# Two first blocks transposed on quarters of the array, and v's conversion moved from GpSimd to VectorE, in a fused attention and MoE kernel

## The chip, the core and the metric

The kernel runs on one core of a Trainium2 chip. The metric is the device time of one execution in microseconds (us), as a median of runs; lower is better. Before the change the three runs gave 338.6, 339.99 and 340.03 us, so the median is 339.99 us.

The engines are named as in the profile: PE is TensorE's matmul, PEld its weight load, DVE is VectorE, ACT is ScalarE, POOL is GpSimd, SP is SyncE, which here only issues DMAs. "SPq" and "POOLq" are the queues of these engines.

## The reference, cut to what matters

q, k and v have 8 batches, 8 heads, 576 positions and 64 channels; f holds forget gates. Attention with a decay is followed by a feed-forward layer of 512 to 2048 to 512 (called MoE in the code):

```python
log_f = np.log(np.clip(f, 0.0001, 1.0))
cum = np.cumsum(log_f, axis=-1)
scores = scale * q @ k.T + cum[:, :, :, None] - cum[:, :, None, :]   # causal
attn = softmax(scores)
x = (attn @ v).transpose(0, 2, 1, 3).reshape(4608, 512)
h = x @ w_in
out = (h * (1.0 / (1.0 + np.exp(-h)))) @ w_out
```

The decay factors into a weight for each key, so the kernel multiplies every row of v (and a column of ones beside it, for the sum of the softmax) by exp(-cum), shifted by half the last sum. That product is what the text calls the conversion of v: it reads fp32 and writes bf16, and it is needed before attention of its batch.

## The kernel before, in words

**Blocks.** A batch's 576 positions are cut into a first block of 128 positions, three blocks of 128 and a tail of 64. First blocks of all 8 batches are done first (a prologue), the rest in the last loop of the kernel, over 16 rounds (`for m in range(NQ)`, L980). This text calls a round a quad; it holds two pairs of heads, n = 2m and 2m + 1, so two quads make a batch: an even one and an odd one. Batch b is attended in quads 2b and 2b + 1.

**First blocks (L131 to L398).** `load_qk0` (L131) has GpSimd load q and k of one first block and cast them to bf16 on the way, one DMA for each, over 128 partitions: a partition holds a run of 8 positions of one head. `turn0` (L285) transposes them with matmuls against a selection matrix `sel` (L293): for q and then for k, 8 positions times 2 halves of heads, 16 matmuls of 64 columns into a PSUM tile of tag "big", each with 128 rows and 64 output partitions. ACT copies q's result out, DVE copies k's (L300). `two_more` (L855) does two first blocks, 4 and 5, then 6 and 7, between pieces of the MoE work. `out0` and `back0` finish a first block.

**The rest.** `load_qk`, `load_tails` and `load_v` (L155 to L194) issue loads, mostly on SP; `load_v(b, c)` loads v's block c + 1 of batch b, so its c = 0 is the first block of the rest, into one of four fp32 buffers vf (L190). `cast_qk` (L402) casts q on POOL, `transposes` (L439) transposes by DMA on SP (L443), and `convert_v(b, c)` (L418) does the conversion of v on POOL (L429): one instruction of 128x520 for c = 0, 1 and 2, and two of 64x260 for c = 3. Each result goes into one of two buffers vp, which take turns by batch.

**A quad (L980 to L1052).** `scores` (L460) computes scores and exponentials, `mask` and `mask_tail` (L490, L496) multiply by triangles on DVE (L492, L498), `attend` (L506) multiplies by v (L522, L531) and DVE normalises (L539, L540). `turn(n)` casts and transposes a later pair and calls `prepare` (L907), which issues the loads of v of the next batch in the even quad and its conversions in the odd quad.

**MoE work in between.** `m1_chunk` (L576) is one chunk hp of the first matmul (4 matmuls L583), followed by a tanh on ACT (L591) and the product gt on DVE (L592). `m2_part` (L610) is a quarter of a row block of the second matmul, po (L628). `m2_rows` (L645) does a whole row block, pr, in row pairs (L654) in two halves, and `m2_fence` (L663) puts a one-column copy of pr on DVE between them (L665); the second half of pr waits for it. All of hp, po, pr, the attention's dn and the transposes share four PSUM buffers of tag "big", which go round in the order of the program; the scores have two buffers of tag "sc".

**The order** is written by hand: every engine runs its instructions in the program's order (`manual_schedule`, L54). `step` (L712) emits a chunk or a part, `wanted` (L695) chooses which, and `fill`, `slot`, `ones` and `rest` emit so many microseconds or so many steps of them.

Of the kernel before, what the change touches and what calls it, by code (L numbers as in the profile page):

```python
# [10 lines left out]
FP32 = mybir.dt.float32  # L11
BF16 = mybir.dt.bfloat16
P = 128
# [5 lines left out]
def kernel(  # L19
# [10 lines left out]
    nc = tc.nc  # L30

    B, H, S, D = q.shape
# [4 lines left out]
    NP = H // 2  # L37
    SM = 512
    ST = S - SM
    NM = SM // P  # L40
# [7 lines left out]
    RUN = 8  # L48
    NRUN = P // RUN
    assert D == 64 and S == 576 and DM == H * D and NP == NCC and B == 8  # L50
    assert NRUN * H == P
    scale = 1.0 / float(D) ** 0.5

    ctx.enter_context(tc.manual_schedule(engines=set(ORDERED)))  # L54
# [13 lines left out]
    psc = ctx.enter_context(tc.tile_pool(name="psc", bufs=2, space=bass.MemoryType.PSUM))  # L68
# [4 lines left out]
    w_bf = const.tile([P, NM + 1, BH], BF16, name="w_bf")  # L73
    ident_bf = const.tile([P, P], BF16, name="ident_bf")
    sel = const.tile([P, 2, D], BF16, name="sel")
    ident_f = const.tile([BH, BH], FP32, name="ident_f")
    tri = const.tile([P, P], BF16, name="tri")
    trit = const.tile([P, 2, ST], BF16, name="trit")
# [4 lines left out]
    kT0 = [const.tile([P, NP, P], BF16, name=f"kT0_{b}") for b in range(B)]  # L83
# [46 lines left out]

    def load_qk0(b):  # L131
        t = conv.tile([P, 2, RUN * D], BF16, name="qkb", tag="qkb")
        for i, src in enumerate((q, k)):
            nc.gpsimd.dma_start(
                out=t[:, i, :],
                in_=src[b, :, 0:P, :].rearrange("h (r c) d -> r h (c d)", c=RUN),
            )
        qk0[b] = t

    def load_v0(b):  # L140
# [277 lines left out]
    def convert_v(b, c):  # L418
        vbf[b] = vps[b % 2]
        if c < NR:  # L420
            parts = [(slice(0, P), slice(0, P), slice(0, H), slice(0, H))]
        else:
            parts = [
                (slice((1 - i) * ST, (2 - i) * ST), slice(ST, P), slice(0, NP), slice(i * NP, (i + 1) * NP))
                for i in range(2)
            ]
        for ro, r, ho, h in parts:
            w = w_bf[r, c + 1, b * H + h.start : b * H + h.stop, None]
            nc.gpsimd.tensor_tensor(  # L429
                out=vbf[b][ro, c, ho, :],  # L430
                in0=vst[b][c][r, h, :],
                in1=w.to_broadcast([r.stop - r.start, h.stop - h.start, D + 1]),
                op=ALU.mult,
            )
# [256 lines left out]
    lag = {"g": 1, "parts": 0}  # L691

    begin: dict[int, tuple[int, int]] = {}

    def wanted(a, c):  # L695

# [15 lines left out]
    def step(force=0):  # L712

        a, c = at["m1"], at["m2"]
        want = wanted(a, c)
        if not want:
            return None
        g1 = M1[a][0] if a < len(M1) else NG
        g2 = M2[c][0] if c < len(M2) else NG
        can1 = g1 in ready and not (M1[a][1] == 0 and g1 > g2 + lag["g"])  # L720
        can2 = open2["w"] and c < len(M2) and g2 < g1
        kind = force if (force == 1 and can1) or (force == 2 and can2) else want
        if kind == 1:
            if M1[a][1] == 0:
                begin[g1] = (0, c)
            m1_chunk(g1, M1[a][1])
            at["m1"] += 1
            t = 4 * (GW[g1] / 2.4 + 2.5)
        else:
            m2_part(*M2[c])  # L730
            at["m2"] += 1
            t = 4 * (DM / 2.4 + 2.5)
        return t

    def behind():
        t = sum(4 * (GW[g] / 2.4 + 2.5) for g, _ in M1[at["m1"] :] if g in ready)
        t += sum(4 * (DM / 2.4 + 2.5) for g, _, _ in M2[at["m2"] :] if g in ready)
        return t / 1000
# [91 lines left out]
        nc.gpsimd.memset(t[:, 0:NM, 1, :], 0.0)  # L830
    load_w_out(0)
    load_w_out(1)
    convert_v0(4)
    convert_v0(5)
    load_w_out(2)
    load_w_out(3)
    load_qk0(6)
    load_qk0(7)
    load_v0(6)
    load_v0(7)  # L840
# [11 lines left out]
    cast_qk(1)  # L852
    transposes(1)

    def two_more(b):  # L855
        for x in range(2):
            turn0(b + x, 0)
            turn0(b + x, 1)
        fill(1.2, 2)
        for x in range(2):  # L860
            scores0(b + x)
            mask0(b + x)
        fill(2.6 if b == 4 else 3.4, 3)
        out0(b)
        fill(0.6, 1)
        out0(b + 1)
        fill(0.8, 2)
        back0(b, on_act)
        fill(0.6, 1)
        back0(b + 1, on_act)  # L870
        if b == 4:
            open2["w"] = True
            step(2)
        else:
            fill(0.6, 1)
# [1 line left out]
    fill(5.9)  # L877
    two_more(4)
    ready.add(1)
    for kind in (1, 1, 2, 1, 1, 2, 1, 1, 1, 1, 2):  # L880
        assert step(kind) is not None
    at["left"] = 0.0
    begin[M1[at["m1"]][0]] = (M1[at["m1"]][1], at["m2"])
    fill(2.2)
    two_more(6)
    ready.add(2)
    store(len(stores))
# [6 lines left out]
    for c in range(NM):  # L894
        convert_v(0, c)
    fill(4.2)

# [9 lines left out]
    def prepare(n):  # L907

        b, p = divmod(n, NP)
        if n != NP - 1 and n + 4 < NU:  # L910
            load_qk(n + 4)
        if b + 1 == B:
            return
        if p == 2 and b + 2 < B:
            load_tails(b + 2)
        if b == 0 and p >= 2 or b > 0 and p == 1:
            for c in range(NM) if b > 0 else range(2 * (p - 2), 2 * (p - 1)):
                load_v(b + 1, c)
        if n == NP - 1:
            load_qk(n + 4)  # L920
        if p >= 2:
            for c in range(2 * (p - 2), 2 * (p - 1)) if b > 0 else range(NM * (p - 2)):
                convert_v(b + 1, c)

    def whole():
# [48 lines left out]
    def slot(us_, least=0, ends=(0, 0)):  # L974
        n = len(stores)
        fill(us_, least, ends)
        store(n)
        passed()

    for m in range(NQ):  # L980
        n = 2 * m
        piece = 1.7 if m < 2 else 2.4
        if m == 2:
            assert at["m2"] >= M2_OF[0]
            first_pool.__exit__(None, None, None)
            gpools[0] = ctx.enter_context(tc.tile_pool(name="third", bufs=1))
            lag["g"] = 2
        if m == 4:
            lag["parts"] = 12
        goal = (spent() if m <= 4 else goal) + QUAD[m]  # L990
        rows = whole()
        late = bool(rows) and m in (1, 3)
        if m < 4:
            store(len(stores))
        scores(n, 0)
        scores(n, 1)
        if m > 0 and not late:
            back(m - 1)
        turn(n)
        if m > 0:  # L1000
            if m % 2 == 0:
                b = m // 2 - 1
                pending.append([1 if m == 2 else 2, [REST_OF[b]] + ([TAILS_OF[b][0]] if b == NM - 1 else [])])
        if rows:
            at["m2"] += 4
            m2_rows(*rows, 0)
            m2_fence(*rows)
            mask(n)
            scores(n, 2)
            scores(n + 1, 0)  # L1010
            turn(n + 1)
            m2_rows(*rows, 1)
            mask_tail(n)
            mask(n + 1)
            scores(n + 1, 1)
            scores(n + 1, 2)
            m2_out(*rows)
            passed()
            attend(n)
            mask_tail(n + 1)  # L1020
            if late:
                back(m - 1)
            if m < 3:
                ones(4 if m < 2 else 3)
            else:
                slot(1.9, 3)
            attend(n + 1)
            if m < 4:
                if m < 3:
                    ones(2 if m < 2 else 4)  # L1030
                else:
                    slot(3.6, 4)
                continue
# [12 lines left out]
        scores(n + 1, 1)  # L1046
        scores(n + 1, 2)
        mask_tail(n + 1)
        slot(piece, 0, (1, 0))
        attend(n)  # L1050
        attend(n + 1)
        slot(min(3.5, max(0.8, behind() - LAG)) if m > 1 else 0.8)  # L1052
    lag["parts"] = 0
    back(NQ - 1)
# [38 lines left out]
```

## Time and profile before

| | before |
|---|---|
| runs | 338.6, 339.99, 340.03 us; median 339.99 |
| profiled execution | 341.14 us |
| its span on the core | 339.4 us |
| PE busy / DVE busy / ACT busy / POOL busy | 326.7 / 200.5 / 217.2 / 139.5 us |
| conversions of v in the rest, on POOL (L429) | 24 of 128x520, mean 1061 ns; 16 of 64x260, mean 697 ns |
| granted clock of TensorE | 0.999 of full |

A line of the timeline has the start and the length in us, the engine, the line of the code, the operation, the tile written and the tiles read, shapes, and how many instructions are merged in it; behind it, in brackets, how long the engine sat idle before it and what ended that wait. A line of the waits has the engine and what it did next, what it waited for, the sum in us, how often and the longest. DMA issues stand under the engine that issues them; a load lands later.

### The profile page before, as it was taken

Reading aid. Unit: us, or ns where it says so; the run is one execution under the profiler, and the core shown is the slowest. Engines: PE = TensorE matmul, PEld = TensorE weight load, DVE = VectorE, ACT = ScalarE, POOL = GpSimd, SP = SyncE. Lnnn points to the kernel's source line nnn. Section 1 sums busy time; section 2 is a strip of 40 time slices with the busy share of each in tenths; the row PEclk is TensorE's granted clock in tenths of the full one; section 3 lists DMA queues with packets and bytes.
Section 4 is the critical chain, followed back from the end, with each engine's and each line's share of the span. In section 5 each row is a group of like instructions: output and inputs, shape, how many; then the busy total and the mean of one; then the engine's idle time right before and its main releaser. Section 6 shows DMA issues by size and latency. Waiting matters only on the chain.

```text
span 339.4 us, 10334 instructions
## 1 busy us (share of the span) xinstructions
PE 326.7 (96%) x4268; PEld 229.2 (68%) x4292; DVE 200.5 (59%) x435; ACT 217.2 (64%) x385; POOL 139.5 (41%) x223
## 2 busy tenths in 40 slices
PE   7999999999999999999999997999999999999995
PEld 3745566798786767758857894867676676555654
DVE  4668745369568467565656965886673557344330
ACT  5767546687777577758748792866776486344431
POOL 8894426574764664464474352628060000000000
PEclk9999999999999999999999999999999999999999
DMA  8999999999999998997999789959973110001012
GB/s 155 187 189 220 180 215 164 241 171 172 182 188 170 168 186 158 194 190 150 181 179 165 147 148 147 156 115 188 151 108 87 53 38 33 34 33 59 34 62 63
DMA packets 144703, 48.01 MB, mean 141 GB/s; under 512 B 133328, under 2 KB 139728, under 8 KB 144656
## 3 DMA queue, kind: packets, MB, share of 16 engines
q1 hardware_dynamic: 115088, 36.60, 56.9%
q0 software_dynamic: 29408, 10.62, 27.0%
q8 instruction: 33, 0.54, 0.7%
q10 hardware_dynamic: 160, 0.13, 0.2%
q14 instruction: 14, 0.11, 0.1%
HBM read 36.85 MB, written 9.44 MB: 136 GB/s over the span
## 4 chain that ended last, share of the span: by engine, by line
PE 85%; DMA 6%; DVE 4%; POOL 2%; issue 1%; ACT 1%; SPq 1%; POOLq 0%
PE hp L583 33%; PE po L628 20%; PE pr L654 15%; PE sc L475 6%; PE dn L522 5%; DMA vf<-in_v_dram 3%; PE dn L531 2%; DMA qkb<-in_k_dram 1%; PE tp L293 1%; DVE gt L592 1%; DMA qf<-in_q_dram 1%; DVE ut L498 1%; DVE u L343 1%; SPq L443 1%; POOL vp L429 1%
## 5 line engine op out<-in xcount | busy, mean ns | idle before, releaser
L591 ACT ACTIVATE th<-hp 128x384 bf16<-128x384 f32 (+2 forms) x208 | 96.5, 468 | 75.0 <-PE hp L583 68.8
L592 DVE SCALAR_TENSOR_TENSOR gt<-th,hp 128x384 bf16<-128x384 bf16 (+2 forms) x208 | 107.5, 523 | 54.3 <-ACT th L591 44.3
L583 PE MATMUL hp<-x,w_in_bf 128*128 128x384 bf16 (+2 forms) x701 | 120.6, 321 | 0.7 <-DVE gt L592 0.4
L583 PEld LDWEIGHTS <-w_in_bf 128*128 128x128 bf16 x832 | 79.0, 98 | 50.2 <-issue 3.7
L486 ACT ACTIVATE u<-sc 128x1024 bf16<-128x1024 f32 (+1 forms) x96 | 74.3, 811 | 6.9 <-PE sc L475 6.9
L628 PE MATMUL po<-w_out_bf,gt 128*128 128x512 bf16 (+1 forms) x316 | 74.1, 368 | 1.4 <-DVE gt L592 0.2
L654 PE MATMUL pr<-w_out_bf,gt 64*128 64x256 bf16 x1024 | 61.4, 269 | 0.0
L409 POOL CAST qkb<-qf 128x384 bf16<-128x384 f32 x32 | 17.3, 542 | 88.9 <-DMA qf<-in_q_dram 88.3
L654 PEld LDWEIGHTS <-gt 64*128 64x128 bf16 x1024 | 51.2, 94 | 3.9
L628 PEld LDWEIGHTS <-gt 128*128 128x128 bf16 x336 | 32.2, 98 | 27.4 <-issue 0.3
L160 POOL DMA_DIRECT2D qkb<-in_k_dram x56 | 43.9, 786 | 0.8 <-issue 0.7
L429 POOL TENSOR_TENSOR vp<-vf,w_bf 128x520 bf16<-128x520 f32 (+1 forms) x40 | 36.5, 915 | 14.0 <-DMA vf<-in_v_dram 11.9
L638 ACT ACTIVATE osb<-po 128x512 f32<-128x512 f32 (+1 forms) x21 | 12.1, 577 | 26.5 <-PE po L628 26.5
L475 PE MATMUL sc<-qkT 64*128 64x128 bf16 (+1 forms) x640 | 28.2, 206 | 0.4 <-DMA qkT<-qkb 0.3
L492 DVE TENSOR_TENSOR u<-u,tri 128x768 bf16<-128x768 bf16 x32 | 20.2, 631 | 13.5 <-ACT u L486 13.5
L475 PEld LDWEIGHTS <-qkT 64*128 64x128 bf16 x640 | 20.3, 94 | 7.6 <-issue 4.7
L480 ACT ACTIVATE ut<-sc 128x640 bf16<-128x640 f32 x32 | 22.4, 701 | 3.0 <-PE sc L475 2.5
L522 PEld LDWEIGHTS <-u 128*128 128x128 bf16 x576 | 20.6, 97 | 3.1
L522 PE MATMUL dn<-vp,u 128*128 128x65 bf16 x384 | 21.8, 193 | 0.0
L540 DVE TENSOR_TENSOR xr<-dn,rec 128x448 bf16<-128x448 f32 x32 | 20.0, 625 | 1.1
L522 PE MATMUL dn<-v,u 128*128 128x65 bf16 x192 | 20.0, 194 | 0.0
L665 DVE COPY fence<-pr 128x1 f32<-128x1 f32 x16 | 2.5, 158 | 28.0 <-PE pr L654 28.0
(70 smaller groups left out, 243.4 us busy)
## 6 DMA issues: line engine op xcount, KB each, us to landing
out_dram<-osb SPq DMA_DIRECT2D x32, 256.0 KB, 2.9
vf<-in_v_dram SPq DMA_DIRECT2D x26, 256.0 KB, 5.1
qf<-in_q_dram SPq DMA_DIRECT2D x64, 96.0 KB, 3.3
qkb<-in_k_dram POOLq DMA_DIRECT2D x56, 48.0 KB, 4.0
w_in_bf<-in_moe_w_in_dram POOLq DMA_DIRECT2D x4, 512.0 KB, 6.8
w_out_bf<-in_moe_w_out_dram POOLq DMA_DIRECT2D x4, 512.0 KB, 9.1
vf<-in_v_dram POOLq DMA_DIRECT2D x6, 256.0 KB, 9.6
qkb<-in_q_dram POOLq DMA_DIRECT2D x8, 128.0 KB, 4.9
```

The lines of the kernel that those rows point to most:

```text
L160: nc.gpsimd.dma_start(out=t2[:, NR + 1 : NX, j * D : (j + 1) * D], in_=k[b, head(p, j), P:SM, :].rearrange("(c p) d -> p c d", p=P),)
L429: nc.gpsimd.tensor_tensor(out=vbf[b][ro, c, ho, :], in0=vst[b][c][r, h, :], in1=w.to_broadcast([r.stop - r.start, h.stop - h.start, D + 1] ...
L475: nc.tensor.matmul(sc[:, i, o : o + q1 - q0], lhsT=kt, rhs=t[r, q0:q1], start=True, stop=True)
L480: nc.scalar.activation(out=ut[:, :, 0:3:2, :].rearrange("p k i t -> p i k t"), in_=sc[:, :, T0 : T0 + (NM + 1) * ST].rearrange("p i (k t) ...
L486: nc.scalar.activation(out=u[:, :, c * SM : c * SM + w], in_=sc[:, :, 0:w], func=ACT.Exp, scale=scale)
L492: nc.vector.tensor_tensor(out=x, in0=x, in1=tri[:, None, None, :].to_broadcast([P, 2, NR, P]), op=ALU.mult)
L522: nc.tensor.matmul(dn[:, i * NR + c - 1, :], lhsT=u[:, i, o : o + P], rhs=vals(kb, i), start=(kb == 0), stop=(kb == c),)
L583: nc.tensor.matmul(hp[:, :], lhsT=w_in_bf[:, cc, fc * P : (fc + 1) * P], rhs=xcols(g, cc), start=(cc == 0), stop=(cc == NCC - 1),)
L591: nc.scalar.activation(out=th[:, :], in_=hp[:, :], func=ACT.Tanh, scale=0.5)
L592: nc.vector.scalar_tensor_tensor(out=gt[:, fc, :], in0=th[:, :], scalar=1.0, in1=hp[:, :], op0=ALU.add, op1=ALU.mult,)
L628: nc.tensor.matmul(po[:, :], lhsT=gt[:, fc, tb * P : (tb + 1) * P], rhs=w_out_bf[:, fc, m0:m1], start=(fc == 0), stop=(fc == NFC - 1),)
L654: nc.tensor.matmul(pos[g, tb][y], lhsT=gt[r, fc, tb * P : (tb + 1) * P], rhs=w_out_bf[r, fc, y * DM // 2 : (y + 1) * DM // 2], start=(half ...
```

## The change

Four things change.

1. First blocks 6 and 7 are loaded with q in partitions 0 to 63 and k in partitions 64 to 127 (four DMAs of 64 partitions for a block instead of two of 128), and transposed by `turn0_quarters`: as many matmuls as before, of 64 rows by 64 output partitions, with q and k and both halves of the heads in different quarters of the array, into a PSUM tile of tag "sc". Both results are evacuated at the end of the block, q's by ACT and k's by DVE. A selection matrix `selh` is built for it by two copies on DVE.
2. GpSimd issues the loads of block 6 earlier, ahead of the conversions of first blocks 4 and 5 and of the last two quarters of w_out.
3. The conversions of v of batches 2 to 7 run on DVE. The one of c = 0 is placed at the start of the odd quad before the batch, ahead of that quad's scores. Those of c = 1, 2 and 3 are put behind the first, third and fifth step of MoE work after the odd quad's last `attend`; what is left over is emitted at the start of the next quad. Batches 0 and 1 stay on GpSimd.
4. Around blocks 6 and 7 the hand-written order of steps has two more chunks ahead of the transposes, `fill(2.2)` becomes `fill(1.8)`, and there is one more step before the loop. The number of chunks and parts is the same in all; a chunk that is done earlier here is missing in quad 1.

```diff
 def load_qk0(b):
     t = conv.tile([P, 2, RUN * D], BF16, name="qkb", tag="qkb")
+    for z, src in enumerate((q, k)):
+        if b < 6:
+            nc.gpsimd.dma_start(out=t[:, z, :], ...)
+            continue
+        for i in range(2):
+            nc.gpsimd.dma_start(
+                out=t[z * D : (z + 1) * D, i, :],
+                in_=src[b, i * NP : (i + 1) * NP, 0:P, :].rearrange(
+                    "a (r c) d -> r a (c d)", c=RUN
+                ),
+            )
...
 def convert_v(b, c):
-            nc.gpsimd.tensor_tensor(
+            (nc.gpsimd if b < 2 else nc.vector).tensor_tensor(
...
 def step(force=0):
...
+        if todo:
+            todo.pop(0)()
         return t
...
     load_w_out(1)
+    load_qk0(6)
     convert_v0(4)
     convert_v0(5)
     load_w_out(2)
     load_w_out(3)
-    load_qk0(6)
     load_qk0(7)
...
+    def turn0_quarters(b):
+        qT0[b] = qktp.tile([P, NP, P], BF16, name="qT0", tag="qT0", bufs=2)
+        sc = psc.tile([P, 2, NP, NRUN, RUN], FP32, name="tq", tag="sc")
+        for c in range(RUN):
+            for j in range(2):
+                for i in range(2):
+                    r = slice(i * D, (i + 1) * D)
+                    nc.tensor.matmul(
+                        sc[j * D : (j + 1) * D, i, :, :, c].rearrange("p a r -> p (a r)"),
+                        lhsT=qk0[b][r, j, c * D : (c + 1) * D],
+                        rhs=selh[r, :],
+                        start=True,
+                        stop=True,
+                    )
+        for i, (dst, evac) in enumerate(
+            ((qT0[b], nc.scalar.copy), (kT0[b], nc.vector.tensor_copy))
+        ):
+            evac(out=dst[...], in_=sc[:, i, :, :, :].rearrange("p a r c -> p (a r c)"))
...
-    for kind in (1, 1, 2, 1, 1, 2, 1, 1, 1, 1, 2):
+    for kind in (1, 1, 2, 1, 1, 1, 1, 2, 1, 1, 1, 1, 2):
         assert step(kind) is not None
...
-    fill(2.2)
+    fill(1.8)
     two_more(6)
...
     fill(4.2)
+    step(1)
...
 def prepare(n):
-        if p >= 2:
-            for c in range(2 * (p - 2), 2 * (p - 1)) if b > 0 else range(NM * (p - 2)):
+        if b == 0 and p == 3:
+            for c in range(NM):
                 convert_v(b + 1, c)
...
+    def later(m):
+        b = m // 2 + 1
+        if m % 2 and 1 < b < B:
+            for c in range(1, NM):
+                todo.extend([lambda b=b, c=c: convert_v(b, c), lambda: None])
...
     for m in range(NQ):
...
         rows = whole()
+        while todo:
+            todo.pop(0)()
+        if m % 2 and 1 < m // 2 + 1 < B:
+            convert_v(m // 2 + 1, 0)
...
         scores(n, 0)
...
             attend(n + 1)
+            later(m)
```

More of the change, by code (lines that the diff above doesn't have):

```diff
@@ L50 @@
     assert D == 64 and S == 576 and DM == H * D and NP == NCC and B == 8
-    assert NRUN * H == P
+    assert NRUN * H == P and NRUN * NP == D
     scale = 1.0 / float(D) ** 0.5
@@ L75 @@
     sel = const.tile([P, 2, D], BF16, name="sel")
+    selh = const.tile([P, D], BF16, name="selh")
     ident_f = const.tile([BH, BH], FP32, name="ident_f")
@@ L132, in load_qk0 @@
         t = conv.tile([P, 2, RUN * D], BF16, name="qkb", tag="qkb")
[L133 to L137, printed above, removed]
+        for z, src in enumerate((q, k)):
+            if b < 6:
+                nc.gpsimd.dma_start(
+                    out=t[:, z, :],
+                    in_=src[b, :, 0:P, :].rearrange("h (r c) d -> r h (c d)", c=RUN),
+                )
+                continue
+            for i in range(2):
+                nc.gpsimd.dma_start(
+                    out=t[z * D : (z + 1) * D, i, :],
[3 more added lines that the diff above has]
+                )
         qk0[b] = t
@@ L693 @@
     begin: dict[int, tuple[int, int]] = {}
+    todo: list = []
     def wanted(a, c):
@@ L853 @@
     transposes(1)
+    for z in range(2):
+        r = slice(z * D, (z + 1) * D)
+        nc.vector.tensor_copy(
+            out=selh[r, :].rearrange("p (a r) -> p a r", a=NP),
+            in_=ident_bf[r, r].rearrange("p (r a) -> p a r", a=NP),
+        )
+    def turn0_quarters(b):
[11 more added lines that the diff above has]
+                        stop=True,
+                    )
+        for i, (dst, evac) in enumerate(
+            ((qT0[b], nc.scalar.copy), (kT0[b], nc.vector.tensor_copy))
+        ):
+            evac(
+                out=dst[:, :, :].rearrange("p a t -> p (a t)"),
+                in_=sc[:, i, :, :, :].rearrange("p a r c -> p (a r c)"),
+            )
     def two_more(b):
         for x in range(2):
-            turn0(b + x, 0)
-            turn0(b + x, 1)
+            if b == 4:
+                turn0(b + x, 0)
+                turn0(b + x, 1)
+            else:
+                turn0_quarters(b + x)
         fill(1.2, 2)
@@ L1051 @@
         attend(n + 1)
+        later(m)
         slot(min(3.5, max(0.8, behind() - LAG)) if m > 1 else 0.8)
```

## The prediction, made before the changed kernel ran

> **What bounds the kernel now.** I read first the busy times and the waits of PE, then the timeline around the longest of them, then the timelines of SP, POOL and DVE around each place where the change puts something.
>
> ```profile
> PE 326.7 (96%) x4268; PEld 229.2 (68%) x4292; DVE 200.5 (59%) x435; ACT 217.2 (64%) x385; POOL 139.5 (41%) x223
> ```
>
> ```profile
> PE hp L583 <- DVE gt L592: 2.6, 3, 2.2
> ...
> PE sc L475 <- DMA qkT<-qkb: 0.3, 1, 0.3
> ...
> PE dn L531 <- POOL vp L429: 0.2, 1, 0.2
> ```
>
> TensorE is the bound: 326.7 of 339.4 us. The 12.7 us left are the first 20 us, the tail, and a handful of waits, of which one is large. The matmul work stays as it is, so the change can only take or give such waits. The large one is in quad 10 (the quads are the 16 rounds of the last loop, from 0), here from three engines' timelines:
>
> ```profile
> 202.99 2.78 DVE L498 TENSOR_TENSOR ut<-ut,trit 128x128 bf16<-128x128 bf16 x1
> ```
> ```profile
> 203.60 2.08 POOL L429 TENSOR_TENSOR vp<-vf,w_bf 128x520 bf16<-128x520 f32 x2
> ```
> ```profile
> 206.15 0.60 PE L583 MATMUL hp<-xt,w_in_bf 128*128 128x256 bf16 x4 [2.24 <-DVE gt L592]
> ```
>
> The small mask (L498) takes 0.22 to 0.23 us elsewhere (127.76, 131.31) and 2.78 here: it ends when POOL's two conversions end. The gate products (gt) queue behind it and PE waits 2.24 us. A second such mask, 2.44 us at 234.88 beside the pair at 235.15, costs nothing, because four-matmul parts of the second matmul (po) stand there that need no DVE.
>
> **Part 1, GpSimd loses the conversions of batches 2 to 7.** 18 of 128x520 and 12 of 64x260 go: 18 x 1.06 + 12 x 0.70 = 27.5 us of POOL. POOL is idle for 88 us waiting for q loads, so its time is worth nothing by itself. The wait in quad 10 goes: **-2.24 us**. Late next there is nothing: without the stall L498 ends at 203.22, the first gt by 203.8, and PE would need it at 203.9. Bounds: 0, if something else held the mask, and -2.24.
>
> **Part 2, VectorE gains them.** DVE has no such row. One conversion reads 520 elements of fp32 and a broadcast weight: the nearest row is the 128x512 product out of PSUM (L382), 691 ns; the half is near the 128x256 one, 423 ns. Bounds for the full one: 0.55 us (the 128x768 bf16 mask with two SBUF inputs, L492) and 1.06 us (GpSimd's own). I take 0.70 and 0.42. Consecutive DVE instructions overlap by some 0.08 us in the timeline (a fence at 126.82 lasting 0.16, the mask behind it at 126.90), so in a full queue a conversion takes 0.62, a 384-wide gt 0.47 instead of 0.55, a 256-wide one 0.34. The halves change partitions and I give them the full 0.42. The three blocks after the first thus add 0.62 + 0.62 + 0.84 = 2.08 us to the MoE stretch of each odd quad from 3 to 13.
>
> A chunk hp may start when the gt four ring places before it is done (tag "big" has 4 buffers), and the next quad's fence (L665) stands behind everything on DVE. Quad by quad, with the gt of before shifted by the conversions in front of them:
> - **Quad 9** is the tight one, eleven chunks 256 wide, at 0.435 us on PE:
>
> ```profile
> 191.34 4.98 PE L583 MATMUL hp<-xt,w_in_bf 128*128 128x256 bf16 x44
> ```
> ```profile
> 192.06 5.14 DVE L592 SCALAR_TENSOR_TENSOR gt<-th,hp 128x384 bf16<-128x384 bf16 x12 [0.15 <-ACT th L591]
> ```
>
>  DVE fills 5.14 us with twelve gt already. The eighth gt would now end at 192.06 + 0.47 + 1.24 + 0.84 + 6 x 0.34 + 0.42 = 197.07; the twelfth chunk needs it and would have started at 191.34 + 10 x 0.435 = 195.69. PE waits **+1.4 us** (+1.2 at the lower bound, +2.1 at the upper).
> - Quad 5: 134.48 + 5 x 0.47 + 2.08 = 138.9 against a fence at 138.86; nothing. Quad 7: 162.61 + 4 x 0.47 + 2.08 = 166.6 against 166.33, but the half of pr behind the fence starts at 166.81; nothing. Quad 3: the pr tile needs the fourth gt at 106.36 + 3 x 0.47 + 1.24 + 0.55 = 109.6, when it is wanted; nothing. Quad 11: the seventh gt at 223.52 + 6 x 0.47 + 2.08 + 0.55 = 229.0 against pr at 228.6; +0.3. Quad 13: the fence waits 4.67 us for PE; hidden. Together **+0.4** with a little for POOL's casts, which still run (a cast at 188.75, 0.50 us, lies beside a mask of 0.45 at 188.88): bounds 0 and 15 conversions x 0.50, of which some 5 would show.
>
> **Part 3, the first block's conversion, placed at the start of each odd quad, ahead of its fence.** This adds a wait for a load at the head of DVE's queue. Behind it stand the fence, the masks and everything after, and the second half of pr (L654) waits for the fence. In quads 5 to 13 v lies there 4 us and more before (POOL takes it at 122.42, the fence is at 126.82) and DVE idles 1.2 to 2.1 us ahead of the fence, which covers 0.70. In **quad 3** it doesn't:
>
> ```profile
> 93.75 5.61 SPq L190 DMA_DIRECT2D vf<-in_v_dram  x4
> ```
> ```profile
> 98.42 0.16 DVE L665 COPY fence<-pr 128x1 f32<-128x1 f32 x1 [1.22 <-PE pr L654]
> ```
> ```profile
> 99.80 1.04 POOL L429 TENSOR_TENSOR vp<-vf,w_bf 128x520 bf16<-128x520 f32 x1 [0.76 <-DMA vf<-in_v_dram]
> ```
>
> Block 0 is issued at 93.75 and lands 5.9 us later, at 99.7: POOL was waiting for it. On DVE the conversion ends at 100.4, the fence at about 100.5, and pr's second half starts then instead of at 98.71: **+1.75 us**. SP's order doesn't change, and SP reaches that load behind POOL's casts and conversions of batch 1, which stay on POOL. Bounds from the landings of these loads (3.6 to 8.0 us): 0 and +3.8.
>
> **Part 4, quarters.** 64 matmuls keep their number, but four small tiles of the array are addressed instead of two. Now:
>
> ```profile
> 47.38 2.08 PE L293 MATMUL tp<-sel,qkb 128*64 128x64 bf16 x64
> ```
> ```profile
> 198.53 0.55 PE L475 MATMUL sc<-qkT 64*128 64x64 bf16 x16
> ```
>
> One start to the next is (2.08 - 0.25) / 63 = 29 ns; the 64-column scores, which already go in row pairs, (0.55 - 0.19) / 15 = 24 ns. At 24 ns: -0.3 us. Bounds: 0, and half the time (-0.93), as pr gains from row pairs (32 of 256 columns in 1.75 us, against 1.74 for 16 of hp). Two copies of 64x64 (selh, some 0.2 us each) stand on DVE ahead of the first gt, where it idles 1.49 us. The evacuations are the same in number and size. The two more DMA issues for each block cost POOL 4 x 0.54 us in all; the four for block 6 lie in its idle 4.42 us before 29.75, and w_out's last two quarters land behind 256 KB more, some 1.4 us at 190 GB/s, with time to spare (33.0 + 8.5 + 1.4 = 42.9 for the last, against a part at 43.8 that is now two 256-wide chunks, 0.87 us, later).
>
> Does that 0.3 reach the end? PE waits at 86.87 for qkT and at 90.51 for vp, at the end of a chain that runs by loads: the third store at SP (56.38 to 59.08) waits for the twelfth po part, then v's blocks 2 and 3 of batch 0 load, POOL converts and casts them (it waits 4.00 us until 64.30), and so on to 90.5. In the new order one more 256-wide chunk (0.435) precedes that part. So the chain moves by +0.435 - 0.3 = **+0.1 us**, and PE's gain turns into a longer wait there. Bounds: -0.5 and +0.45.
>
> **Sum:** -2.24 + 1.4 + 0.4 + 1.75 + 0.1 = +1.4 us. The profiled execution took 341.14 us (span 339.4 and 1.7 around it), so 342.5 by its own time; it lay 1.15 above the median of the runs, 339.99, and on that footing I say **341.4**.
>
> **Rivals.**
> - *The waits don't show.* v lands in time in quad 3 (loads have landed in 3.6 us) or quad 9's queue drains faster: 339.6 without quad 3's wait, 338.2 without either, 337.6 if the quarters pass half their time on. For it: DVE is 59% busy. Against it: POOL's 0.76 us wait for that very load.
> - *DVE is held by POOL, slower.* A conversion on DVE has two SBUF inputs, like the masks that POOL held at 202.99 and 234.88. If each late conversion waits for one cast (0.50 us), the odd quads lose 1.5 us each; it decides from 0.1 us on, since quads 5, 7 and 11 have no more spare, so 3 x 1.5 and 1.5 more in quad 9: 341.4 + 6 = 347.4, half of that, 344.4, if every second one meets a cast. For it: the mask at 188.88; against it: a mask of 0.56 at 113.52 beside POOL issuing DMAs.
>  The Trainium skill, "GPSIMD Engine Reference", Key points, says that GpSimd shares its SBUF interfaces with VectorE and contends with VectorE instructions that have two SBUF inputs. By that rule the held mask is rightly put down to POOL, and the moved conversions bring the same exposure to DVE; the trace agrees on the masks and can't show the conversions.
> - *The change doesn't remove the wait in quad 10.* The mask began at 202.99 while POOL's row still shows DMA issues until 203.58. If those held it, the 2.24 stays: 343.6.
>
> **Chances.** Forecast (340.4 to 343) 0.45, of it 0.30 within 0.5% (about what a measurement of this kernel can tell from no change: 338.3 to 341.7) and 0.15 slower. No waits 0.30: 0.22 faster, 0.08 within. Held by POOL 0.15, slower. Wait stays 0.10, slower. Faster 0.22, same 0.38, slower 0.40. The range takes in quad 3's load at its late end (+2 more) and the quarters with no waits: 337.4 to 345.0, leaving out the worse half of the second rival.
>
> **What would show it.** Right: no PE wait near 205; a fence in quad 3 that waits for a conversion, which waits for DMA vf; a 1 to 2 us wait of hp for gt in quad 9; conversions on DVE of about 0.70; the 64 quarter matmuls in 1.5 to 1.6 us, with longer waits at 86 to 90. Wrong: conversions over 0.9 us, waits of PE in quads 5, 7 or 11 over 0.5 us, or v of batch 2 landing before 98.

## The result, and the profile after

The changed kernel takes 344.01 us (median of 6 runs, 341.37 to 346.64) against 339.64 us (6 runs, 338.6 to 340.05): a ratio of 1.0111, 95% interval 1.008 to 1.0142, so it is 1.1% slower. The ratios here and below leave out runs more than 1.5% above the fastest of their kernel (346.64 here, and 346.27 in one experiment); without it the median here is 343.5 us. The profiled execution is the longest of its runs: 346.64 us, span 344.9, mean granted clock 0.995. In the other runs the clock was 1.0 (341.37), 0.999 (342.96), and 0.994 or 0.995 in the rest.

Lines move down by 10 from where the prediction gave them: the fence is L675, pr L664, hp L593, gt L602, the small mask L508, the conversion L439, v's loads L200. From the page of the changed kernel, the busy times and the clock:

```profile
PE 329.9 (96%) x4269; PEld 230.0 (67%) x4292; DVE 208.4 (60%) x467; ACT 217.4 (63%) x385; POOL 115.6 (34%) x197
...
PEclk9999999999998999999999999999999999999999
```

POOL is 23.9 us less busy, DVE 7.9 more (17.9 of conversions, and 6.1 less of small masks). PE is 3.2 us *more* busy though it has no more to do. A lower clock does that, but this row can't show it so finely, as a second profile of the kernel before (below) has 330.0 at a whole clock. The clock's own row is better: its one 8 stands near 105 us. Now PE's waits (in total, times, longest):

```profile
PE pr L664 <- DVE fence L675: 2.7, 1, 2.7
...
PE hp L593 <- DVE gt L602: 1.2, 3, 0.6
...
PE sc L485 <- ACT u L496: 1.1, 1, 1.1
PE dn L541 <- POOL vp L439: 0.5, 1, 0.5
```

The 2.24 us in quad 10 is gone. The largest wait is new: pr behind the fence, once. That is quad 3, here on SP, DVE and PE (the first line is the wait of scores, 1.1 in the list above, which stands in quad 2):

```profile
86.95 0.40 PE L485 MATMUL sc<-qkT 64*128 64x128 bf16 x8 [1.06 <-ACT u L496]
```
```profile
94.78 6.11 SPq L200 DMA_DIRECT2D vf<-in_v_dram  x4
```
```profile
101.22 0.70 DVE L439 TENSOR_TENSOR vp<-vf,w_bf 128x520 bf16<-128x520 f32 x1 [3.59 <-DMA vf<-in_v_dram]
101.84 0.15 DVE L675 COPY fence<-pr 128x1 f32<-128x1 f32 x1
```
```profile
102.04 3.12 PE L664 MATMUL pr<-w_out_bf,gt 64*128 64x256 bf16 x32 [2.71 <-DVE fence L675]
```

The load is issued at 94.78 and its first block lands 6.4 us later; DVE sits 3.59 us with the conversion at the head of its queue; the fence runs only then, and PE has nothing for 2.71 us. The 32 matmuls then take 3.12 us, not the 1.92 they take elsewhere in the two profiles. The windows (length; PE busy and its groups; granted clock; DMA share; GB/s) show why:

```profile
100.00:102.00 2.00, 0.00 (x0) 1.00 1.18 135
102.00:104.00 2.00, 1.96 (x24) 0.64 1.26 128
104.00:106.00 2.00, 2.00 (x31) 0.50 1.04 284
106.00:108.00 2.00, 2.00 (x40) 1.00 1.59 197
```

Behind the idle stretch TensorE gets half its clock for over 3 us: 2 x 0.36 + 2 x 0.50 = 1.7 us of full-speed work is lost on top of the wait. The fences tell how that adds up: they come at 64.8, 86.4, 98.4, 111.4 and 246.0 (quads 0, 2, 3, 4, 13) before, and at 65.1, 85.7, 101.8, 117.2 and 251.6 after. So the difference is +0.3, -0.7, +3.4, +5.8 and +5.6: nearly all of it seems made between the fences of quads 2 and 4: 4.1 us up to the fence of quad 3 (2.9 of them its delay, and 1.1 longer waits of scores and dn in quad 2) and 2.3 behind it. From quad 4 to quad 15 the two kernels take the same, 165.5 and 165.4 us. But this profile of before holds the 2.24 us wait in quad 10; the second profile of before takes 163.0, so some 2.3 us of the loss lie there as well. The new conversions themselves and the small masks on DVE (count, total us, mean ns), and quad 9:

```profile
L439 DVE TENSOR_TENSOR vp<-vf,w_bf 128x520 bf16<-128x520 f32 x18 | 12.8, 713 | 3.6 <-DMA vf<-in_v_dram 3.6
L508 DVE TENSOR_TENSOR ut<-ut,trit 128x128 bf16<-128x128 bf16 x32 | 8.0, 251 | 3.3 <-ACT ut L490 3.2
L439 DVE TENSOR_TENSOR vp<-vf,w_bf 64x260 bf16<-64x260 f32 x12 | 5.1, 426 | 0.3
```
```profile
199.46 1.03 PE L593 MATMUL hp<-xt,w_in_bf 128*128 128x256 bf16 x8 [0.34 <-DVE gt L602]
200.73 1.03 PE L593 MATMUL hp<-xt,w_in_bf 128*128 128x256 bf16 x8 [0.24 <-DVE gt L602]
202.41 1.47 PE L593 MATMUL hp<-xt,w_in_bf 128*128 128x256 bf16 x12 [0.65 <-DVE gt L602]
```

PE waits 1.23 us for gt in quad 9, as its ring of four buffers said. Last, the quarters, and the moved loads on POOL:

```profile
48.10 1.09 PE L882 MATMUL tq<-selh,qkb 64*64 64x64 bf16 x64
```
```profile
30.54 0.50 POOL L142 DMA_DIRECT2D qkb<-in_k_dram  x1 [2.06 <-DMA w_in_bf<-in_moe_w_in_dram]
```

64 matmuls on quarters take 1.09 us where they took 2.08. And POOL, issuing the fourth load of block 6, stands 2.06 us until an earlier DMA of its queue is done; what it issues behind that is 1.6 us later than before (w_out's third quarter 33.86 against 32.20). This lateness isn't the stand's alone: in the second profile of the changed kernel POOL stands 2.10 us at the same place and issues that quarter at 32.56.

### The profile page after: what moved, and what is told of

The parts are those of the page before. It is cut to its first block, busy times and chain, and to the rows that moved or that the text cites. A ratio compares the mean times of both kernels' runs of the same rounds, so it can differ in the third digit from the quotient of the medians.

```text
span 344.9 us, 10351 instructions
## 1 busy us (share of the span) xinstructions
PE 329.9 (96%) x4269; PEld 230.0 (67%) x4292; DVE 208.4 (60%) x467; ACT 217.4 (63%) x385; POOL 115.6 (34%) x197
## 4 chain that ended last, share of the span: by engine, by line
PE 78%; DMA 10%; DVE 3%; POOL 2%; SPq 2%; issue 1%; ACT 1%; POOLq 0%; DVEq 0%
PE hp L593 28%; PE po L638 20%; PE pr L664 14%; DMA vf<-in_v_dram 7%; PE sc L485 6%; PE dn L532 5%; DMA qf<-in_q_dram 3%; PE dn L541 2%; DVE gt L602 2%; PE wm L250 1%; DVE vp L439 1%; SPq L453 1%; POOL v L358 1%; ACT th L601 1%; SPq L179 1%
## 5 line engine op out<-in xcount | busy, mean ns | idle before, releaser
L602 DVE SCALAR_TENSOR_TENSOR gt<-th,hp 128x384 bf16<-128x384 bf16 (+2 forms) x208 | 106.4, 522 | 53.6 <-ACT th L601 45.8
L593 PE MATMUL hp<-x,w_in_bf 128*128 128x384 bf16 (+2 forms) x701 | 120.9, 321 | 0.4
L593 PEld LDWEIGHTS <-w_in_bf 128*128 128x128 bf16 x832 | 78.9, 98 | 49.9 <-issue 3.3
L664 PE MATMUL pr<-w_out_bf,gt 64*128 64x256 bf16 x1024 | 63.2, 272 | 3.2 <-DVE fence L675 2.7
L664 PEld LDWEIGHTS <-gt 64*128 64x128 bf16 x1024 | 52.4, 95 | 8.0 <-issue 3.5
L502 DVE TENSOR_TENSOR u<-u,tri 128x768 bf16<-128x768 bf16 x32 | 20.1, 629 | 14.1 <-ACT u L496 14.0
L439 DVE TENSOR_TENSOR vp<-vf,w_bf 128x520 bf16<-128x520 f32 (+1 forms) x30 | 17.9, 598 | 3.9 <-DMA vf<-in_v_dram 3.6
L593 PE MATMUL hp<-xt,w_in_bf 128*128 128x256 bf16 x128 | 16.9, 272 | 1.2 <-DVE gt L602 1.2
```

The costliest lines, as they stand in the source:

```text
L439: (nc.gpsimd if b < 2 else nc.vector).tensor_tensor(out=vbf[b][ro, c, ho, :], in0=vst[b][c][r, h, :], in1=w.to_broadcast([r.stop - r.start ...
L502: nc.vector.tensor_tensor(out=x, in0=x, in1=tri[:, None, None, :].to_broadcast([P, 2, NR, P]), op=ALU.mult)
L593: nc.tensor.matmul(hp[:, :], lhsT=w_in_bf[:, cc, fc * P : (fc + 1) * P], rhs=xcols(g, cc), start=(cc == 0), stop=(cc == NCC - 1),)
L602: nc.vector.scalar_tensor_tensor(out=gt[:, fc, :], in0=th[:, :], scalar=1.0, in1=hp[:, :], op0=ALU.add, op1=ALU.mult,)
L664: nc.tensor.matmul(pos[g, tb][y], lhsT=gt[r, fc, tb * P : (tb + 1) * P], rhs=w_out_bf[r, fc, y * DM // 2 : (y + 1) * DM // 2], start=(half ...
```

## The experiments

Ratios are to the kernel before, run on the same chip among the same runs; its median was 339.03, 339.11 and 339.51 us in the three sets.

The theory after this profile: the fence that waits for a load in quad 3, with the clock's fall behind it, makes most of the loss, and the early loads on POOL add to it by making v late. The rivals: DVE is loaded in every odd quad, by conversions or by contention; or the quarters and the new early order cost the time.

### Block 0 of batch 2 converted later

```
 def later(m):
-    for c in range(1, NM):
+    for c in range(0 if b == 2 else 1, NM):
...
-if m % 2 and 1 < m // 2 + 1 < B:
+if m % 2 and 2 < m // 2 + 1 < B:
     convert_v(m // 2 + 1, 0)
```

> The changed kernel, but in quad 3 alone the conversion of v's block 0 (batch 2) stands behind attend, at the head of the list that the MoE steps take up, and not ahead of the fence. Theory (the fence that waits for a load in quad 3 makes most of the loss): the 2.71 us wait of pr and the low clock behind it go (2 us at 0.64 and 2 us at 0.50 lose 1.7 us of full-speed work), and one more 0.70 us conversion in quad 3's chunks costs 0.3 at most. From 344.0 that leaves 339.6 to 340.1, within 0.2% of the kernel before, with a granted clock of 0.998 or more in every run. Rival A (conversions on DVE load every odd quad): 343 to 344, as 27 of 30 conversions stay where they are. Rival B (the quarters and the early order make it): 343 to 344.

Measured: 340.55 us (339.11 to 342.9, 9 runs), 1.0051 (1.003 to 1.0072), with a clock of 0.999 or 1.0 in every run. The theory's place is right: over the kernel before of its own set the changed kernel lost 3.9 us (343.5 against 339.64) and 2.8 when measured again (below), and 1.5 are left here, so 1.3 to 2.3 us go by moving one instruction of 0.70 us. But 1.5 us stay, more than the 0.1 to 0.6 I had left for the rest, so the loss isn't in quad 3's fence alone.

### The quarters alone

```
-(nc.gpsimd if b < 2 else nc.vector).tensor_tensor(
+nc.gpsimd.tensor_tensor(
```
and the conversions called where the kernel before calls them.

> The kernel before with the part on quarters alone: quarters for blocks 6 and 7, their loads at the new place, the new order of early MoE steps; all conversions of v stay on GpSimd. Theory: PE's starts after the wait at 90.95 were 0.44 us later than before, so about 340.1 against 339.6; the 2.24 us wait in quad 10 stays. My prediction had +0.1 for this part (339.7). Rival B (the early order makes the loss): 342 or more, with a wait of 1 us and more at 86 to 91 that is not made up. Rival C (the quarters' gain of 1 us on PE is kept): 338.8.

Measured: 337.65 us (337.05 to 338.26, 6 runs), 0.9956 (0.9941 to 0.9971). Of what was written down, none had it: theory and prediction had a small loss, and the gain passes even the rival that keeps all of PE's 1 us (338.8 from its footing of 339.6; 338.0 from the 339.03 of this set). Half of the change is a gain of 1.4 us. Where my prediction had a chain of loads that PE's gain would run into at 86 to 91, the profile has PE waiting 0.8 us there and still 1.6 us ahead at the fence of quad 3 (96.8 against 98.4): in this execution the chain came earlier too. SP issues v's four loads of batch 2 at

```profile
92.19 5.20 SPq L200 DMA_DIRECT2D vf<-in_v_dram  x4
```

against 93.75 before.

### The conversions alone

Quarters, loads and early order as before; conversions as in the change.

> The kernel before with the conversions of v of batches 2 to 7 on DVE alone: first blocks turned as before, loads and early steps in the old order. Theory: the wait in quad 3 stays (v's block 0 is issued near 93.75 again and PE is there 0.44 us earlier too, so 2 to 3 us) and with it the fall of the clock where the wait passes some length: 342 to 343.7. By the prediction's own sum for this part, +1.3: 340.9, with a wait of 1.75. Rival B: 339.6 to 340.2.

Measured: 343.27 us (340.3 to 344.95, 6 runs), 1.0104 (1.0067 to 1.0141). So the conversions cost 4.2 us by themselves, and the quarters by themselves gain 1.4. The profiled run was the fastest of them, 340.3, and in it v's block 0 landed 4.3 us after its issue at 92.41 and PE didn't wait for the fence at all. The runs spread over 4.6 us with a clock of 0.998 or more in each: a length of wait that differs from run to run, at the fence or in quad 2, not the clock, is what is left to explain that. It is argued, as only one of them has a profile.

### The loads of block 6 at their old place

```
-    load_qk0(6)
     convert_v0(4)
...
     load_w_out(3)
+    load_qk0(6)
```

> The changed kernel with the four loads of block 6 back behind the last quarter of w_out. Theory: POOL's wait of 2.06 us for a DMA slot at 30.54 goes, convert_v0(4) begins near 29.75 again, the 0.90 us wait of dn at 32.94 goes, and SP's chain is about 1 us earlier; PE's own gain is 0.4 at most, but v of batch 2 lands about 1 us earlier too, so the wait in quad 3 is 1.6 to 2.7. 341.5 if the clock then stays whole, 343.5 if it falls as before. Rival (the early place of the loads matters to nothing late): 344, wait 2.7.

Measured: 341.32 us (6 runs, 340.57 to 346.27); 1.0062 (1.004 to 1.0084). In the profile POOL's wait of 2.06 us is gone, SP issues v at 92.44, block 0 lands 4.6 us later, and PE waits 0.25 us for the fence, not 2.71. But two other stands have come on POOL, 2.33 and 2.60 us at loads of block 7, and the quarter matmuls wait 0.85 us for them. The time is that of the better outcome expected; the cause is not shown, as this is one profile of a wait that varies, and SP issued v at 92.14 in another run with the loads at the early place (PE kept busy in quad 3, below). The run at 346.27 had a clock of 0.995.

### The kernel before, profiled again

> The kernel before, unchanged, profiled a second time: does the 2.24 us wait of PE in quad 10 belong to every execution? By the prediction's part 1 it does: PE waits 2.2 us for gt near 205 again, span near 339. By the other reading, born of the quarters-only run, whose mask in quad 10 took 0.22 us with the same two GpSimd conversions behind it (they began 0.6 us after the mask had begun): the mask is held only where those conversions begin just while it runs, the wait is absent here, and the span is 337 to 337.5.

Measured: one run of 340.44 us, span 338.7. PE doesn't wait in quad 10. (It waits 1.8 us for qkT in two places, 1.35 of it at 88.72, where the first profile has 0.3; hence the span.) The mask and POOL in this profile, and then in that of the quarters alone:

```profile
204.78 0.22 DVE L498 TENSOR_TENSOR ut<-ut,trit 128x128 bf16<-128x128 bf16 x1
```
```profile
205.35 1.07 POOL L429 TENSOR_TENSOR vp<-vf,w_bf 128x520 bf16<-128x520 f32 x1
```
```profile
201.43 0.22 DVE L508 TENSOR_TENSOR ut<-ut,trit 128x128 bf16<-128x128 bf16 x1
```
```profile
202.03 2.08 POOL L439 TENSOR_TENSOR vp<-vf,w_bf 128x520 bf16<-128x520 f32 x2
```

In the prediction's profile the mask began at 202.99 and the pair at 203.60, 0.61 us apart; here 0.57 and 0.60. At the same distance to 0.01 us the mask took 2.78 us in one execution and 0.22 in another. The pair is batch 6's, converted early. In the four profiles besides the first that have it on GpSimd and no gaps put in, the mask took 0.21 or 0.22. So the wait that the prediction takes away isn't a property of the kernel: one execution of five had it. That the pair does hold a mask is well supported all the same. Beside such pairs in quads 10 and 12, four masks of the ten in these five profiles take over 2 us: two in the first, and one each in quad 12 of two runs with the quarters alone. Here the later of the two, with the loads at the old place:

```profile
232.16 2.77 DVE L508 TENSOR_TENSOR ut<-ut,trit 128x128 bf16<-128x128 bf16 x1
```
```profile
232.76 2.07 POOL L439 TENSOR_TENSOR vp<-vf,w_bf 128x520 bf16<-128x520 f32 x2
```

Each of the four ends 0.1 us after its pair. They began 0.27 to 0.61 us ahead of it, and the six that were not held 0.44 to 0.86, so the distance doesn't decide; what does stays open.

### PE kept busy in quad 3

```
     turn(n + 1)
+    if m == 3:
+        keep_warm(11)
     m2_rows(*rows, 1)
```

> The changed kernel with 11 matmuls of 512 columns on zeros (0.215 us each, 2.4 us; they add nothing to the output) on PE in quad 3 between the small scores and the second half of pr, so that PE is busy while the fence is awaited. Theory (the clock falls because of PE's idle stretch there): every run has a clock of 0.998 or more, no slice at 0.5 behind the fence, the wait itself shrinks to 0.1 to 0.5 us but pr starts no earlier; 342 to 343.5, and no run above 345. Rival (the fall has another cause): 2 or more of the runs at 0.995 again, and over 344.

Measured: 342.48 us (341.73 to 343.12, 6 runs), 1.0096 (1.0077 to 1.0115), every clock 0.998 or more. As the theory said: in its profile DVE waits 3.08 us for the load, PE's idle stretch is filled, pr's half takes 1.92 us and the clock stays at 1.00 in every window from 98 to 106. The clock alone proves little here, since it stayed whole in most runs of the changed kernel when measured again without the filler (below). The spread shrinks to 1.4 us; that the filler does it by fixing the wait's length is argued. It is no gain on the median of the changed kernel in the last set (342.31, below).

### Quad 9's conversions moved

Block 0 of batch 2 as above, and batch 5's block 2 at the start of quad 10, its tails behind that quad's first mask:

```
+if m == 10:
+    convert_v(5, 2)
...
 mask(n)
+if m == 10:
+    convert_v(5, 3)
```

> The run with block 0 of batch 2 moved, and besides v's block 2 of batch 5 converted at the start of quad 10 (0.70 us in DVE's idle 1.46 us ahead of the fence) and its tails (0.86 us) behind the first mask of quad 10. Theory: of quad 9's waits of hp for gt (0.34, 0.24, 0.65) the second and third go, -0.9 us, and nothing comes in their place: 339.6 against 340.55 without this move. Rival (the loss of these conversions is spread over all odd quads or over late loads): within 0.3 of 340.55.

Measured: 339.1 us (338.06 to 340.39, 12 runs), 0.9993 (0.9973 to 1.0014). Against 340.55 that is -1.45 (the two were measured in different sets). In the profile two of the three waits are gone, as expected:

```profile
193.46 3.22 PE L593 MATMUL hp<-xt,w_in_bf 128*128 128x256 bf16 x28 [0.34 <-DVE gt L602]
```

With both places mended the conversions on DVE still are 1.45 us behind the quarters alone (337.65, another set).

### Idle stretches of set lengths

Multiplications of a tile of zeros on DVE ahead of eight fences of the kernel before.

```
+for _ in range({4: 5, 5: 7, 7: 8, 8: 9, 10: 10, 11: 11, 13: 13, 14: 15}.get(m, 0)):
+    nc.vector.tensor_tensor(out=warm[:, :], in0=warm[:, :], in1=warm[:, :], op=ALU.mult)
 m2_fence(*rows)
```

> The kernel before with 5, 7, 8, 9, 10, 11, 13, 15 multiplications of a 128x512 tile of zeros by itself (about 0.4 us each) on DVE ahead of the fences of quads 4, 5, 7, 8, 10, 11, 13, 14, so that PE idles there for lengths from about 0.5 to 4 us; the output is the same. Asked: from which idle stretch on does the granted clock fall, and for how long. Theory: the stretches under about 2 us leave it at 1.0, those from 2.7 us on are followed by 2 to 4 us at about half. Rival: a stretch has no effect, or only where it is over 3.4 us, and the fall in quad 3 had another cause.

Measured: 374.02 us, one run. The same 32 matmuls behind stretches of six lengths (the two left out are 5.92 again, and 1.64 with 1.92):

```profile
115.11 2.90 PE L654 MATMUL pr<-w_out_bf,gt 64*128 64x256 bf16 x32 [2.11 <-DVE fence L665]
133.17 1.92 PE L654 MATMUL pr<-w_out_bf,gt 64*128 64x256 bf16 x32 [0.74 <-DVE fence L665]
162.75 1.92 PE L654 MATMUL pr<-w_out_bf,gt 64*128 64x256 bf16 x32 [1.28 <-DVE fence L665]
176.83 3.17 PE L654 MATMUL pr<-w_out_bf,gt 64*128 64x256 bf16 x32 [2.62 <-DVE fence L665]
214.04 2.85 PE L654 MATMUL pr<-w_out_bf,gt 64*128 64x256 bf16 x32 [3.13 <-DVE fence L665]
236.69 3.60 PE L654 MATMUL pr<-w_out_bf,gt 64*128 64x256 bf16 x32 [5.92 <-DVE fence L665]
```

Read the duration and the bracket: up to 1.64 us the half takes 1.92; from 2.11 on it takes 2.85 to 3.60, and the windows give 0.50 for some 3.4 us, that is 1.7 us of full-speed work lost, behind 2.11, 2.62 and 3.13 (0.72, 0.50 and 0.93 in the three windows of 2 us from 115 on). So an idle stretch does bring the clock down, and the rival with 3.4 us falls.

### The changed kernel again

> The changed kernel, unchanged, on the chip and among the runs of the others of this set, with a second profile. Theory: the time is set by when v's block 0 of batch 2 lands in quad 3, so runs spread from about 341 to 346.6, median 343 to 344.5, those above 344 with a clock of 0.996 or less. The parts do not add up (quarters alone -1.4, conversions alone +4.2, sum 341.8): with the quarters PE and DVE reach the fence's place earlier, while the load comes no earlier. Rival (the parts add up, and the difference was between chips): 341.8.

Measured: 342.31 us (340.84 to 343.61, 10 runs), 1.0087 (1.006 to 1.0113). Lower than I expected, and nearer to the sum of the parts (341.8): that the parts hinder each other isn't shown. Two of ten runs had a clock of 0.995, against four of six at first, and they weren't the longest (341.2 and 343.28). The kernel before, which has no such wait at the fence, shows 0.995 or less in 11 of its 64 runs beside the three sets, so a run's mean clock doesn't tell what happened in quad 3. The profile is the telling part:

```profile
100.63 1.93 PE L664 MATMUL pr<-w_out_bf,gt 64*128 64x256 bf16 x32 [2.62 <-DVE fence L675]
```

The wait is there again, nearly as long, v's block 0 having landed 6.4 us after its issue at 93.45; but the half takes 1.93 us. The clock did not fall.

### The quarters alone, loads at the old place

> The quarters-only kernel with the loads of block 6 back behind w_out's last quarter. In the changed kernel that place gave 341.3 against 344.0, which I put down to the fence of quad 3. If the gain came by that fence alone, it is absent here, where GpSimd converts: 337.3 to 338.5 (-0.3 from POOL's wait at 28.68 going, +0.8 from quarter matmuls that wait for the later load, as in that run). Rival (POOL's early waits for slots cost a microsecond or more on their own): 336.5 or less.

Measured: 338.45 us (336.5 to 340.06, 12 runs), 0.9964 (0.9933 to 0.9995). In its profile the quarter matmuls wait 1.6 us for a load of k, which now is issued behind more. Whether the early place is better for the quarters isn't settled: 0.9964 here against 0.9956 with the early place and the same order of steps, and the intervals overlap (337.71 below has the old order). The rival, 336.5 or less, is out; that the early place costs the changed kernel time by the fence is argued from these runs, not shown.

### DVE for four batches only

```
-(nc.gpsimd if b < 2 else nc.vector).tensor_tensor(
+(nc.vector if b in (3, 4, 6, 7) else nc.gpsimd).tensor_tensor(
```
and the calls to match.

> The changed kernel with batches 2 and 5 left on GpSimd: DVE converts v in quads 5, 7, 11 and 13 only (20 of the 30 conversions). Theory (the loss sits in quads 3 and 9, where a load comes late and where DVE has 256-wide chunks to serve): 337.65 of the quarters-only kernel plus 0.2 to 0.5 for quad 11, so 337.8 to 338.3, faster than the kernel before by 0.2 to 0.4%. Rival (each quad with conversions on DVE loses alike): two thirds of the loss remain, 339.5 or more.

Measured: 338.56 us (337.78 to 339.97, 12 runs), 0.9965 (0.9943 to 0.9987). A little over what the theory gives, and well under the rival: 20 of 30 conversions cost 0.9 us against the quarters alone, the other 10 cost 3.75 more (342.31). The profile agrees: from the fence of quad 4 to that of quad 15 it takes 163.79 us, against 163.02 with the quarters alone (old order) and 165.34 with all 30.

### The quarters alone, early steps in the old order

> The quarters-only kernel with the early MoE steps in the old order (the list of eleven steps, 2.2 and no step more at the end); quarters and their loads stay. Asked: is the gain of 1.4 us that of the quarter matmuls (1.09 us on PE against 2.08 in the profiles) or that of the new order? If that of the quarters: 337.6 to 338.1. If the new order was needed to keep it, because the old one leaves PE waiting at 86 to 91 for what was loaded: 338.6 to 339.2, the prediction's picture of that stretch.

Measured: 337.71 us (336.6 to 338.38, 12 runs), 0.9946 (0.9925 to 0.9967). The same as with the new order, so the new order isn't needed for the gain. The quarter matmuls themselves save 0.99 us of PE; where the rest of the 1.4 to 1.8 comes from isn't shown. With the quarters alone above, this is the best version found; it beats both kernels.

## Why the prediction came out as it did, step by step

The forecast of 341.4 with slower as its likeliest sign was right in sign, and the 344.01 (342.31 in the second measurement) lies inside the wide range of 337.4 to 345.0; only the second measurement lies inside the narrow one, 340.4 to 343. The forecast change was +1.4 us, the measured one +3.9 (343.5 against 339.64) and +2.8. Two of the steps were wrong by about 2 us each, in opposite directions; that they largely offset each other is luck. What is left of the miss is a longer wait in quad 3, the fall of the clock there, and quads 9 and 11.

- **The wait in quad 10, -2.24: failed.** The step took a wait of one execution for a cost of the kernel. The second profile of before and three other kernels with those conversions on GpSimd don't have it. It also spoiled the footing: I took the median of 339.99 as if it held the wait, though the profiled run lay 1.15 above it, which was the sign. Four of five profiles give it a value of 0.
- **Quarters, +0.1: failed.** Matmuls on quarters take half as long (1.09 us, at the end that I bounded by -0.93, and not 24 ns each). The step then let PE's gain turn into a longer wait at 86 to 91. That happened in some executions (waits of 1.06 and 0.54 us in the changed kernel, 1.10 and 0.50 in its second profile) and not in others (0.45 us in all with the old order); the kernel before has 0.28 and 0.18 in one profile and 1.35 in the other. SP issued v of batch 2 at 91.5 to 94.8 in the ten profiles with quarters and at 92.4 to 95.5 in three without. So the profiles spread too much to show a chain that eats the gain, and the runs say that it is kept: -1.4 and -1.8.
- **Quad 3, +1.75: right in mechanism, short in the profile.** The wait was 2.71 and 2.62 us in two profiles of the changed kernel, 0.25 and none where the load landed in 4.3 to 4.6 us instead of 6.4. Between runs, moving the instruction away is worth 1.3 or 2.3 us. The fall of the clock, 1.7 us more where it came, wasn't in the prediction at all.
- **Quad 9, +1.4: right in place, a little short.** PE's waits for gt are 1.23 us in the profile; from fence to fence the quad is 1.71 longer, inside the bounds of 1.2 to 2.1.
- **The other quads, +0.4: too small.** By runs, 0.9 us for quads 5, 7, 11 and 13 together. The fences place it: quad 11 is 0.59 us longer, quad 7 0.27, and quad 3 0.4 even where neither the wait nor the clock counts. The waits of pr for gt name only 0.2 to 0.4 us of that.
- **The durations, 0.70 and 0.42: right** (0.713 and 0.426). The loads of block 6 on POOL "in its idle 4.42 us": right in place, but POOL's queue stood some 2.1 us there for a DMA to finish; in the second profile the conversion behind it begins at 29.61, against 29.75 before.

The distances between fences in the profiles, in us, show the losses without the spread of the runs:

| from fence to fence, quads | before | before, again | quarters alone, old order | changed | changed, again |
|---|---|---|---|---|---|
| 2 to 3 | 11.98 | 12.98 | 11.80 | 16.11 | 16.02 |
| 3 to 4 | 12.97 | 12.97 | 12.97 | 15.31 | 13.37 |
| 9 to 10 | 14.26 | 14.26 | 14.26 | 15.97 | 15.97 |
| 10 to 11 | 17.31 | 14.92 | 14.92 | 14.92 | 14.92 |
| 11 to 12 | 14.53 | 14.53 | 14.53 | 15.12 | 15.12 |
| 4 to 15 | 165.52 | 163.03 | 163.02 | 165.36 | 165.34 |

The last line gives the conversions 2.3 us behind quad 4 in both profiles of the changed kernel. With 0.4 in quad 3, a wait at the fence that delays it by 2.8, and -1.6 for the quarters, the second profile should lie 3.9 us over the kernel before; it took 343.26 us against 339.51, 3.75 more. The median of its runs is 2.8 over; that the load came sooner in most of them is argued, as only one has a profile. The first line is the unsteady one: without any conversion on DVE in quad 3 (DVE for four batches only) it still took 14.36 us once, by waits in quad 2.

That DVE is held by POOL was not the cause: of the 18 large conversions one takes 1.03 us and the others 0.69 or 0.70. The masks gain. The 32 small masks took 14.1 us before and 8.0 after; over all profiles 9.2 to 14.1 with the conversions on GpSimd and 7.1 to 8.1 with those of batches 2 to 7 on DVE. That agrees with what the prediction cites of the Trainium skill, "GPSIMD Engine Reference", Key points; but that relief was off PE's path in most executions.

## What to carry to other kernels

Before a wait seen in a profile is counted as a gain, look for it in a second execution, or ask whether the runs' median already lies below the profiled time. An instruction that waits for a load costs what stands behind it in its engine's queue, so ask of a moved one whether its data is there in the late case, and put it behind the short thing that another engine needs (here a 0.15 us fence). And judge the halves of a change apart: this one held a gain of 1.4 us and a loss of 4.2.

## What the runs showed of the hardware

- **The clock falls behind short idle stretches, but not always.** PE stretches of 0.74, 1.28 and 1.64 us left it at 1.00; 2.11, 2.62, 2.71 and 3.13 were followed by 0.50 for some 3.4 us, 5.92 by 0.50 for over 5; 2.24 (before, quad 10) and 2.62 (the changed kernel again) were not. The Trainium skill, "TensorE: Matmul & The Clock Gate", section "Why this matters for your kernels", warns of idle gaps of over some 3 us. These runs have it from 2.11 us on. Its section "What's actually happening" has the clock judged by a window that runs free of the program; that one length falls in one execution and not in another would fit such a window, but no run here shows it.
- **Matmuls of 64x64 by 64 columns on four quarters** follow each other faster than half-array ones: 64 in 1.09 us against 64 in 2.08.
- **Two engines at the same distance, two outcomes:** the small mask 0.6 us ahead of GpSimd's two conversions took 2.78 us in quad 10 of one execution and 0.22 in another; held masks end 0.1 us after the second conversion.
- **One load's landing varied** from 4.3 to 6.5 us after its issue, between kernels and executions that move the same data. With it the fence's wait went from 0 to 2.7 us; in part this came from the issue, which was 2.1 us ahead of pr's first half in the two profiles with the long wait and 2.7 to 2.8 in the two with the short.
